# Full attention layers: one of a quad's 32 exponential tiles computed on VectorE and POOL instead of ScalarE

## The chip, the core and the metric

One core of a Trainium2 chip. The metric is the time of one launch in device microseconds. The engines are named as the profile names them: PE (matrix products), PEld (its weight loads), DVE (VectorE), ACT (ScalarE), POOL (GpSimd) and SP (SyncE, which issues the DMAs).

## What is computed

Four layers of pre-norm attention with a residual, on 2048 rows of width 512, 32 heads of width 16, all in float32: layers 0 and 2 look at the 256 rows up to their own (windowed), layers 1 and 3 at all rows (full).

```python
def _B_ref(x, wqkv, wo):            # _A_ref: the same with a mask of W = 256
    qkv = (lambda x, *d: x.transpose(*d))((x @ wqkv).reshape(B, S, 3, H, Dh), 2, 0, 3, 1, 4)
    q, k, v = qkv[0], qkv[1], qkv[2]
    scores = jnp.einsum("bhqd,bhkd->bhqk", q, k) * scale
    p = _softmax(scores, axis=-1)
    o = jnp.einsum("bhqk,bhkd->bhqd", p, v)
    return (lambda x, *d: x.transpose(*d))(o, 0, 2, 1, 3).reshape(B, S, D) @ wo

x = A_x
x = x + _A_ref(_layernorm(x, axis=-1), A_wqkv, A_wo)
x = x + _B_ref(_layernorm(x, axis=-1), B_wqkv, B_wo)
x = x + _A_ref(_layernorm(x, axis=-1), A_wqkv, A_wo)
x = x + _B_ref(_layernorm(x, axis=-1), B_wqkv, B_wo)
```

## The kernel before

The work of a full layer is cut into 32 quads: four blocks of 512 query rows (c) by eight groups of four heads (qd). Layer 1 takes the blocks one after the other with all eight groups of each; layer 3 takes two groups of every block, then the next two. A quad meets its 2048 keys in 16 steps j of 128 keys (`attn_full`, L767). A step makes two tiles of scores, one for each pair of heads: a tile is 128 keys by two heads by 512 queries, 128x1024 numbers.

- `exps` (L718): eight matmuls (L727) write a tile of scores into a PSUM buffer; there are two such buffers (`ps_s`). ACT takes the exponential into an SBUF tile e (L735); there are six of these (EB). A shift that keeps the exponent in range is part of the operands, as an added row of q and of k, so there is no running maximum.
- `pv` inside `attn_full` (L779): the value product of a step, called PV below, multiplies both tiles of the step with the values and adds into the two banks `acc`. A column of ones in the values gives the softmax's denominator.
- `epilogue` (L681): when a quad's last PV is done, DVE takes `acc` to SBUF (the tile sa, by `join`, L415 and L416), transposes, divides, and every second quad splits the result into two float16 halves (POOL takes one subtraction, L712). The next quad's first PV starts `acc` anew and so waits for sa.

Between these matmuls PE does **side work**: the projections of queries, keys and values, and the output product, of this layer or the next. They run as groups of eight matmuls of 64 rows (`mms`, L390, L399) into the one remaining PSUM bank pair, called halves, b in the rows of the profile. A chain of such groups (12 for a tile of 128x512 in most cases) ends with `join` on DVE, which frees the bank for the next chain. Query and key projections also square their result (POOL, L521), sum the squares (L543) and take a maximum (L562) or a shift (L575, L576).

The order of PE's and DVE's instructions in full layers is written by the program itself, in the order of a simulated clock kept in Python: a step counts 1.8 us, a group of side work MM = 0.222 us, DVE's backlog is kept in `vt_`. `share` (L949) deals out side work by a budget: after the second scores of a step one to two groups, as long as the clock allows. Light DVE work is queued by `soon` and issued by `drain` when DVE is thought to be free. `flush` (L738) decides when a PV is emitted: a step's PV comes two steps' scores later, between the two scores of a step, because `attn_full` hands control back (`yield None`) after its first tile and `attention` (L986) then calls `flush(1)`. ACT's and SP's instructions are placed by the framework's scheduler.

A quad's operands are the query tile qt (two buffers, L748) and two halves of the keys kt (three buffers, L752); `attention` loads a quad's operands while the one ahead runs, but not across the end of a block.

The memory rings that matter below: `vw` has three buffers (VB) and holds side work's weights and layer 2's value tiles (L623); `xh` has four (XNB).

Of the kernel before, what the change touches and what calls it, by code (L numbers as in the profile page):

```python
# [33 lines left out]
EB, XB, XNB, WB, VB, OB = 6, 4, 4, 2, 3, 5  # L34
RINGS = WB, VB
L_MIN = 2.0 ** -90
# [153 lines left out]
def fast_path(ctx, tc, flag, a_x, a_wqkv, a_wo, b_wqkv, b_wo, out):  # L190
# [13 lines left out]
    ctx.push(ps_x)  # L204
    dp = pool("scr", 1, space=bass.MemoryType.DRAM)
# [5 lines left out]
    XC, XN, V, O, OT, KM, PH = {}, {}, {}, {}, {}, {}, {"free": 0.0, "busy": False}  # L211
    WT, ST, pend = {}, {}, []
    VQ, vt_ = [deque() for _ in range(4)], [0.0]
# [15 lines left out]
    def soon(chain, us, f):  # L229

        if PH["full"]:
            VQ[chain].append((clock[0], us, f))
        else:
            f()

    def drain(upto=None):

        if upto is not None:
            for q in VQ[:upto]:
                while q:  # L240
                    vec(q[0][1])
                    q.popleft()[2]()
            return
        while vt_[0] <= clock[0] + 0.2:
            q = next((q for q in VQ if q), None)
            if q is None:
                return
            vec(q[0][1])
            q.popleft()[2]()
# [21 lines left out]
    zeros = cp.tile([P, QC], F16, name="zeros")  # L271
# [15 lines left out]
    nc.gpsimd.memset(zeros, 0.0)  # L287
# [15 lines left out]
    def fill(t, key, c0=0, c1=1):  # L303
        r4 = lambda d0, d1: rows(t).rearrange("h (d b) (c n) -> h d b c n", b=4, n=QC)[:, d0:d1, 3]
        for c in range(c0, c1):
            if key:
                nc.sync.dma_start(r4(0, 1)[:, 0, c], ones[:H])
                nc.sync.dma_start(r4(1, DH)[:, :, c], zeros[:H, None, :].broadcast_to([H, DH - 1, QC]))
# [33 lines left out]
    def verify(ty, s):  # L342

        am = vp.tile([P, D], F32, name=f"wa{ty}_{s}", tag="wa", bufs=1)
        for k in range(NC):
# [4 lines left out]
            yield from turns(3, (1.1, lambda: nc.vector.tensor_reduce(am[:, f], raw.rearrange("p k f -> p f k"), axis=AX.X, op=ALU.max,  # L350
                                                                      apply_absolute_value=True)))

        def bounds():
            at = vp.tile([P, D], F32, name=f"wt{ty}_{s}", tag="wc", bufs=1)
            nc.vector.transpose(at, am)
            mx = vp.tile([P, D // 32], F32, name=f"wx{ty}_{s}", tag="wx")
            nc.vector.tensor_reduce(mx, at.rearrange("p (b r) -> p b r", r=32), axis=AX.X, op=ALU.max)
            nc.vector.tensor_tensor(wlow, wlow, mx, ALU.min)
            nc.vector.tensor_tensor(whigh, whigh, mx, ALU.max)
        yield from turns(3, (1.8, bounds))  # L360
# [12 lines left out]
    def phase(l):  # L373

        PH["full"], PH["win"] = l is not None and l % 2 == 1, l is not None and l % 2 == 0
# [53 lines left out]
    def norm(l, c, xs, tail=False):  # L429

        mv, y, nb, out = ST[l, c][1], [], [], []

        def scales():
            y.append(rsqrt(nc, vp, f"{l}_{c}", mv[:, :, 1]))
# [4 lines left out]
        def parts(i):  # L439
            xn = vp.tile([P, D], F32, name=f"xn{l}_{c}_{i}", tag="xn", bufs=1)  # L440
# [12 lines left out]
        yield from turns(2, (2.4, scales), *[(1.8, lambda i=i: parts(i)) for i in range(4)])  # L453
# [24 lines left out]
    def project(l, s, c, act, ht=None):  # L478
# [5 lines left out]
        xc = XC[l, c]  # L484
        if s == 0:
# [6 lines left out]
        for t in range(NHT) if ht is None else (ht,):  # L492
# [19 lines left out]
            def parts(t=t, sp=None if full else sp, j=j if full else None):  # L512
                if full:
                    sp = vp.tile([P, 2, QC], F16, name=f"sp{n}_{t}", tag="sp", bufs=3)
                    nc.vector.tensor_copy(sp[:, 0], j)  # L515
                    nc.vector.tensor_tensor(sp[:, 1], j, sp[:, 0], ALU.subtract)
                sq = vp.tile([P, QC], BF16, name=f"sq{n}_{t}", tag="sq", bufs=NHT)
# [47 lines left out]
    def queries(l, c, act, ht=None):  # L565
        sqs = yield from project(l, 0, c, act, ht)

        def rest():
# [3 lines left out]
            if l % 2:  # L572
                r = quarters(ht)
                if PH["full"]:
                    nc.vector.tensor_scalar(m[r], ph[r, 0], -0.515, None, op0=ALU.mult)  # L575
                    nc.vector.scalar_tensor_tensor(m[r], ph[r, 1], -0.515, m[r], op0=ALU.mult, op1=ALU.add)  # L576
                else:
                    nc.vector.tensor_scalar(m[r], ph[r], -0.515, None, op0=ALU.mult)
# [16 lines left out]
    def key_shift(l, ht=None):  # L595
# [6 lines left out]
        nc.vector.tensor_scalar(m[r], ones[r], kx[r], -0.515, op0=ALU.mult, op1=ALU.mult)  # L602
# [4 lines left out]
    def values(l, c, act, halves=(0, 1), tiles=range(4)):  # L607
# [14 lines left out]
        else:  # L622
# [19 lines left out]
    def wo(l, c, tail):  # L642
# [17 lines left out]
        if PH["full"]:  # L660
            yield from norm(l + 1, c, xs, tail)
# [19 lines left out]
    def epilogue(l, c, qd, a):  # L681
# [33 lines left out]
        if u:  # L715
            soon(1, 1.2, parts)
# [524 lines left out]
```

## Time and profile before

| | |
|---|---|
| median of 3 runs | 2761.76 us (2757.35 to 2763.62) |
| the profiled execution | 2759.5 us, of which the span from the first to the last instruction 2757.7 us |
| busy in that span | PE 2496.1, ACT 2362.9, DVE 1094.9, PEld 1100.3, POOL 515.8 us |
| granted TensorE clock | 0.988 of full |
| layer 1, layer 3 | from about 500 to 1448 us, from about 1790 to 2741 us |
| DMA | 359.67 MB, mean 130 GB/s |

A row of the profile's groups reads: line, engine, operation, tile written <- tiles read, partitions x elements, count | busy time, mean length of one in ns | idle time of the engine in front of them, and what ended it. A row of the order of time reads: start, length, engine, line, operation, tiles, count, and in brackets the idle time ahead with what ended it; rows of one kind that follow each other without a break are merged, so "x8 ... 0.41" is eight matmuls from the start of the first to the end of the last. PE's matmuls overlap; the time that a group takes is read from start to start.

### The profile page before, as it was taken

The numbers are of one execution on the slowest core, as the hardware profiler recorded it, in microseconds if no ns is written. First come the engines' busy times: TensorE is split into PE (matmuls) and PEld (weight loads), VectorE is DVE, ScalarE is ACT, GpSimd is POOL, SyncE is SP. The second block draws the span as 40 slices with busy tenths as digits, with TensorE's granted clock in tenths as the row PEclk, the third lists the DMA queues.
The fourth block names the chain that finished last, engine by engine and source line by source line (L and its number), as shares of the span: only waits on it lengthen the run. The fifth ranks groups of instructions, "written<-read, shape, count | busy, mean of one in ns | idle before, by whom it ended". The sixth has DMA issues, their size and how long they took to land.

```text
span 2757.7 us, 112292 instructions
## 1 busy us (share of the span) xinstructions
PE 2496.1 (91%) x50513; PEld 1100.3 (40%) x50513; DVE 1094.9 (40%) x2314; ACT 2362.9 (86%) x2683; POOL 515.8 (19%) x1074
## 2 busy tenths in 40 slices
PE   7888989999989999999998898899899999998987
PEld 3233334444433344444443333534444444433332
DVE  5564554122343335325326566323333333333333
ACT  4556654899999999999995667399999999999997
POOL 1445552001000000100105678100000000000000
PEclk9999999999999999999999999999999999999999
DMA  8888856322342224324225565623232333333332
GB/s 286 226 241 240 244 178 191 96 83 82 100 120 79 86 93 137 102 78 126 93 73 169 157 181 143 175 72 109 84 107 90 98 97 104 112 104 123 114 120 103
DMA packets 335035, 359.67 MB, mean 130 GB/s; under 512 B 113616, under 2 KB 250320, under 8 KB 328144
## 3 DMA queue, kind: packets, MB, share of 16 engines
q1 hardware_dynamic: 334544, 352.40, 42.3%
q8 instruction: 397, 6.50, 1.0%
q14 instruction: 94, 0.77, 0.1%
HBM read 239.60 MB, written 96.99 MB: 122 GB/s over the span
## 4 chain that ended last, share of the span: by engine, by line
ACT 56%; PE 23%; issue 11%; DVE 5%; DMA 3%; POOL 2%; SPq 0%; ACTq 0%; DVEq 0%; POOLq 0%
ACT e L735 55%; PE b L402 10%; PE acc L812 3%; PE acc L779 3%; PE bs L402 2%; PE s L731 2%; PE s L727 2%; PE b L399 1%; POOL e L802 1%; POOL e L805 1%; DMA qt<-qs 1%; DMA kt<-kw 0%; DMA wr<-in_A_wo_dram 0%; DVE ot L694 0%; DMA w<-wd 0%
## 5 line engine op out<-in xcount | busy, mean ns | idle before, releaser
L735 ACT ACTIVATE e<-s 128x1024 f32<-128x1024 f32 (+2 forms) x2432 | 2238.8, 1058 | 121.0 <-PE s L731 95.3
L779 PE MATMUL acc<-e,vt 64*17 64x512 f32 x16384 | 1085.0, 590 | 1.3 <-issue 1.3
L727 PE MATMUL s<-qt,kt 64*32 64x512 f16 x16384 | 849.0, 380 | 130.4 <-ACT e L735 106.6
L727 PEld LDWEIGHTS <-kt 64*32 64x32 f16 x16384 | 406.7, 89 | 944.2 <-issue 868.8
L779 PEld LDWEIGHTS acc<-e,vt 64*17 64x17 f32 x16384 | 280.5, 92 | 61.1 <-issue 1.5
L805 POOL TENSOR_SCALAR_AFFINE_SELECT e<-e 128x256 f32<-128x256 f32 x512 | 224.9, 446 | 196.5 <-ACT e L735 195.4
L802 POOL TENSOR_SCALAR_AFFINE_SELECT e<-e 128x256 f32<-128x256 f32 x448 | 198.1, 449 | 114.1 <-ACT e L735 112.3
L712 POOL TENSOR_TENSOR oh<-o,oh 128x512 f16<-128x512 f32 x31 | 36.1, 1165 | 938.1 <-DVE oh L711 884.8
L812 PE MATMUL acc<-e,vt 128*17 128x384 f32 (+2 forms) x2816 | 204.7, 396 | 5.3 <-POOL e L802 4.0
L731 PE MATMUL s<-qt,kt 64*128 64x384 f16 (+2 forms) x1408 | 129.0, 280 | 64.0 <-ACT e L735 38.2
L415 DVE TENSOR_SCALAR sa<-acc 128x512 f32<-128x512 f32 x64 | 44.3, 692 | 335.4 <-PE acc L779 335.4
L402 PE MATMUL b<-xc,w 128*128 128x512 f16 x696 | 166.1, 390 | 7.0 <-DMA w<-wd 5.8
L677 DVE SCALAR_TENSOR_TENSOR x<-b,x 128x512 f32<-128x512 f32 x122 | 83.9, 688 | 193.0 <-PE b L399 189.8
L402 PEld LDWEIGHTS <-w 128*128 128x128 f16 x816 | 77.4, 100 | 122.8 <-issue 35.8
L521 POOL TENSOR_TENSOR sq<-sp 128x512 bf16<-128x512 f16 x28 | 41.0, 1463 | 442.2 <-DVE sp L515 427.6
L506 ACT ACTIVATE sp<-b 128x512 f16<-128x512 f32 x58 | 34.7, 598 | 103.3 <-PE b L402 91.2
L731 PEld LDWEIGHTS <-kt 64*128 64x128 f16 x1408 | 54.4, 94 | 167.6 <-issue 137.0
L521 POOL TENSOR_TENSOR sq_h<-sp_h 128x512 bf16<-128x512 f16 x27 | 40.1, 1484 | 409.8 <-DVE sp_h L515 409.8
L399 PE MATMUL b<-wo,oh 64*32 64x512 f16 x2592 | 109.9, 376 | 6.2 <-DVE x L677 3.1
L399 PE MATMUL b<-xc,w 64*32 64x512 f16 x2688 | 110.9, 376 | 3.0 <-DVE j L416 2.3
L399 PE MATMUL b<-xc,w_h 64*32 64x512 f16 x2592 | 104.4, 376 | 4.1 <-DVE km L562 3.9
L415 DVE TENSOR_SCALAR j_h<-b 128x512 f32<-128x512 f32 x27 | 18.7, 691 | 218.7 <-PE b L399 187.6
(136 smaller groups left out, 1874.8 us busy)
## 6 DMA issues: line engine op xcount, KB each, us to landing
kt<-kf SPq DMA_DIRECT2D x128, 512.0 KB
qt<-qs SPq DMA_DIRECT2D x128, 256.0 KB
xd<-x SPq DMA_DIRECT2D x96, 256.0 KB
x<-xd SPq DMA_DIRECT2D x96, 256.0 KB
w<-wd SPq DMA_DIRECT2D x22, 1024.0 KB
kt<-kw SPq DMA_DIRECT2D x64, 256.0 KB
qs<-sp SPq DMA_DIRECT2D x48, 256.0 KB
wo<-wd SPq DMA_DIRECT2D x12, 1024.0 KB
```

What stands on the lines that cost most here:

```text
L399: nc.tensor.matmul(ps[g:g + 32, r], a[k, g:g + 32], b[k], start=(i == 0), stop=(i == len(pairs) - 1), skip_group_check=True)
L402: nc.tensor.matmul(ps, a, b, start=(i == 0), stop=(i == len(pairs) - 1))
L415: nc.vector.tensor_scalar(dst, ps[0], scale, None, op0=ALU.mult)
L521: nc.gpsimd.tensor_tensor(sq, sp[:, 0], sp[:, 0], ALU.mult)
L677: nc.vector.scalar_tensor_tensor(xs[i], p, 1 / WS, xs[i], op0=ALU.mult, op1=ALU.add)
L727: nc.tensor.matmul(ps[g:g + 32, h], kt[R * h:R * h + R, pr, kc + g:kc + g + 32], qt[R * h:R * h + R, pr], start=True, stop=True, skip_grou ...
L731: nc.tensor.matmul(ps[:, h, s0:s0 + wd_], kt[R * h:R * h + R, pr, kc:kc + P], qt[R * h:R * h + R, pr, qc:qc + wd_], start=True, stop=True)
L735: nc.scalar.activation(e[:, :, w0:w1], ps[:, :, w0:w1], AF.Exp, scale=SCALE)
L779: nc.tensor.matmul(acc[r][32 * h:32 * h + DH + 1, :], V[l, qd // 4, j // 8][k, j % 8, 4 * (qd % 4) + h, :], es_[h // 2][k, h % 2, :], star ...
L802: nc.gpsimd.affine_select(v, v, pattern=[[0, 2], [-1, P]], compare_op=ALU.is_gt, fill=0.0, base=0, channel_multiplier=1)
L805: nc.gpsimd.affine_select(v, v, pattern=[[0, 2], [1, P]], compare_op=ALU.is_ge, fill=0.0, base=0, channel_multiplier=-1)
L812: nc.tensor.matmul(a[32 * h:32 * h + DH + 1, q * P:(q + nb) * P], V[l, (4 * c + j) // 4][:, j % 4, 4 * qd + h, :], es_[h // 2][:, h % 2, s ...
```

## The change

One tile of each quad, the first head pair of step 7 (`DJ`), no longer goes through ACT. It is called a unit. Its scores are written into the side work's bank (`unit`). DVE takes them from there, scaled by log2(e) and as whole numbers with 23 binary places, into an SBUF tile d; then it cuts out the fraction (two operations into a scratch tile) and the exponent bits (in place in d). POOL evaluates a polynomial of degree five in the fraction, ten operations for each half of 512, in five pieces, and multiplies d by it. The program decides in `units` when a unit is issued: at the earliest 6 us of its clock after its operands' load, when POOL has little left. The shift of the scores is changed so that they stay negative (L605 after the change).

Step 7 is moved to the end of the quad, so that its PV finds d ready. In the moved step only the second pair goes through ACT.

Further parts:
- e has five buffers in full layers instead of six (`EB = (6, 5)`); d has two.
- The scratch tile of the polynomial takes a buffer of `vw` in layer 1 and all of `xh` in layer 3. In layer 1 no unit is issued once layer 2's third value tile begins (`PH["off"]`).
- POOL's order, too, is written by the program in full layers (`PQ`, `pt_`).
- The next quad's operands are loaded across the end of a block (`fetch`).
- The planner: projections wait until the squares of the one ahead are due (`PH["sq"]`), up to two or three groups of side work between scores (`share`), and the split of the output waits for a free buffer (`OFREE`).
- The test of the weights' range is done in four pieces of 128 columns.

```diff
-EB, XB, XNB, WB, VB, OB = 6, 4, 4, 2, 3, 5
+EB, XB, XNB, WB, VB, OB = (6, 5), 4, 4, 2, 3, 5
+DJ = NT // 2 - 1
+TS, TT = 0.6, 1.25
+XP = 10 * (TS + TT)
...
+            if PH["full"] and c == 2:
+                PH["off"] = True
+                finish_unit()
             vt = V[l, c] = wp.tile([P, 4, H, DH + 1], F32, name=f"vt{n}", tag="vw", bufs=VB)
...
+    def unit(u):
+
+        ps = PH["halves"]
+        for g in range(0, P, 32):
+            for h in range(2):
+                nc.tensor.matmul(ps[g:g + 32, h], u["kt"][R * h:R * h + R, 0, DJ % 8 * P + g:DJ % 8 * P + g + 32],
+                                 u["qt"][R * h:R * h + R, 0], start=True, stop=True, skip_group_check=True)
+        spent(0.27)
+        vec(1.4)
+        PH["free"] = max(clock[0] + 0.6, vt_[0])
+        t = PH["ep"].tile([P, 2, QC], I32, name=f"d{u['n']}", tag="d", bufs=2)
+        nc.vector.tensor_scalar(t, ps, SCALE * LOG2E * 2.0 ** 23, -2.0 ** 30, op0=ALU.mult, op1=ALU.max)
...
+        def bits():
+            for h in range(2):
+                nc.vector.tensor_scalar(f[h].bitcast(I32), t[:, h], 0x7FFFFF, 0x3F800000, op0=ALU.bitwise_and, op1=ALU.bitwise_or)
+            nc.vector.tensor_scalar(t, t, 0x3F800000, None, op0=ALU.bitwise_and)
+            pt_[0] = max(pt_[0], vt_[0])
+            for k in range(5):
+                PQ.append((2 * (TS + TT), lambda k=k: horner(k)))
+
+        def horner(k):
+            for h in range(2):
+                if k:
+                    nc.gpsimd.tensor_scalar(a[h], a[h], POLY[4 - k], None, op0=ALU.add)
+                else:
+                    nc.gpsimd.tensor_scalar(a[h], f[h], POLY[5], POLY[4], op0=ALU.mult, op1=ALU.add)
+            for h in range(2):
+                if k < 4:
+                    nc.gpsimd.tensor_tensor(a[h], a[h], f[h], ALU.mult)
+                else:
+                    nc.gpsimd.tensor_tensor(x[:, h], a[h], x[:, h], ALU.mult)
+                    u["done"] = True
...
     def attn_full(l, c, qd, kt, qt, a):
-        for j in range(NT):
+        js = [j for j in range(NT) if j != DJ] + [DJ]
+        for j in js:
             es_ = []
-            for pr in range(2):
+            if j == DJ:
+                u = UX.popleft()
+                es_ = list(u["e"])
+                if es_:
+                    finish_unit() if UX and not UX[0]["e"] or not UX else None
+            PH["step"] = 1.8 - 0.9 * len(es_)
+            for pr in range(len(es_), 2):
                 es_.append(exps(f"{l}_{c}_{qd}_{j}_{pr}", kt[j // 8], qt, pr, [(j % 8 * P, 0, QC, 0)]))
                 if pr == 0:
                     yield None
...
-            self.lag = max(self.lag - 0.42, -0.3)
+            self.lag = max(self.lag - 0.48, -0.4)
...
-                   and self.spent - s0 < 1.5 * MM):
+                   and self.spent - s0 < (1.5 if self.lag > 0.1 else 2.5) * MM):
```

How it moves instructions, at three places. The first is PE at the end of a quad of layer 1 (s_1_2_15_1: scores of block 1, quad 2, step 15, pair 1; s_1_3_0_0: the next quad's first). One row of each group of eight or four matmuls is shown. Before:

```order
L727 MATMUL s_1_2_15_1_13728<-qt_1_2_12382,kt_1_2_1_12386 32x512
L727 MATMUL s_1_3_0_0_13745<-qt_1_3_13088,kt_1_3_0_13090 32x512
L779 MATMUL acc_81<-e_1_2_14_0_13678,vt_0_1_5232 17x512
L727 MATMUL s_1_3_0_1_13769<-qt_1_3_13088,kt_1_3_0_13090 32x512
L779 MATMUL acc_81<-e_1_2_15_0_13713,vt_0_1_5232 17x512
L727 MATMUL s_1_3_1_0_13793<-qt_1_3_13088,kt_1_3_0_13090 32x512
```

And after the change, at the same place:

```order
L767 MATMUL s_1_2_15_1_13888<-qt_1_2_12564,kt_1_2_1_12568 32x512
L767 MATMUL s_1_2_7_1_13923<-qt_1_2_12564,kt_1_2_0_12566 32x512
L767 MATMUL s_1_3_0_0_13950<-qt_1_3_13245,kt_1_3_0_13247 32x512
L892 MATMUL acc_81<-e_1_2_14_0_13842,vt_0_1_5228 17x512
L892 MATMUL acc_81<-e_1_2_15_0_13878,vt_0_1_5228 17x512
L767 MATMUL s_1_3_0_1_13987<-qt_1_3_13245,kt_1_3_0_13247 32x512
L892 MATMUL acc_81<-d_1_2_12947,vt_0_0_4499 17x512
L892 MATMUL acc_81<-e_1_2_7_1_13932,vt_0_0_4499 17x512
L767 MATMUL s_1_3_1_0_14011<-qt_1_3_13245,kt_1_3_0_13247 32x512
```

Step 7's one score tile stands between step 15's and the next quad's, and two PVs (of steps 14 and 15) stand between the next quad's first two score tiles, where one stood. This is so at all 31 places between two quads of a full layer.

The second place is PE at the end of layer 1 (quad 3_7 is its last; s_0_0_0_0 is layer 2's first score tile). Before:

```order
L727 MATMUL s_3_7_15_1_28645<-qt_3_7_27293,kt_3_7_1_27297 32x512
L779 MATMUL acc_81<-e_3_7_14_0_28605,vt_1_1_5653 17x512
L779 MATMUL acc_81<-e_3_7_15_0_28635,vt_1_1_5653 17x512
L731 MATMUL s_0_0_0_0_28701<-qt_0_0_28694,kt_0_0_28693 128x384
```

After; the rows left out are 288 matmuls of layer 2's third value projection, b<-wv_2_0_0,xc_2, in three chains:

```order
L767 MATMUL s_3_7_15_1_29212<-qt_3_7_27838,kt_3_7_1_27842 32x512
L767 MATMUL s_3_7_7_1_29223<-qt_3_7_27838,kt_3_7_0_27840 32x512
...
L892 MATMUL acc_81<-e_3_7_14_0_29163,vt_1_1_5656 17x512
L892 MATMUL acc_81<-e_3_7_15_0_29202,vt_1_1_5656 17x512
L892 MATMUL acc_81<-d_3_7_28184,vt_1_0_5831 17x512
L892 MATMUL acc_81<-e_3_7_7_1_29232,vt_1_0_5831 17x512
L771 MATMUL s_0_0_0_0_29585<-qt_0_0_29578,kt_0_0_29577 128x384
```

The projection that ran among the quads of layer 1 now stands for the most part behind their last scores.

The third is POOL, which runs a unit's chain without other work in between (here layer 3's second one; scr_0 and scr_1 hold the fraction, scr_2 and scr_3 the polynomial); DVE's part of another unit stands below it:

```order
L808 TENSOR_SCALAR scr_2_33926<-scr_0_33924 128x512
L808 TENSOR_SCALAR scr_3_33927<-scr_1_33925 128x512
L811 TENSOR_TENSOR scr_2_33926<-scr_2_33926,scr_0_33924 128x512
L811 TENSOR_TENSOR scr_3_33927<-scr_3_33927,scr_1_33925 128x512
L806 TENSOR_SCALAR scr_2_33926<-scr_2_33926 128x512
L806 TENSOR_SCALAR scr_3_33927<-scr_3_33927 128x512
...
L813 TENSOR_TENSOR d_0_1_34497<-scr_2_33926,d_0_1_34497 128x512
L813 TENSOR_TENSOR d_0_1_34497<-scr_3_33927,d_0_1_34497 128x512
L551 TENSOR_TENSOR sq_1_0_h_1_34999<-sp_1_0_h_1_34996 128x512
```

```order
L789 TENSOR_SCALAR d_1_4_46951<-b_33923 128x1024
L797 TENSOR_SCALAR scr_0_33924<-d_1_4_46951 128x512
L797 TENSOR_SCALAR scr_1_33925<-d_1_4_46951 128x512
L798 TENSOR_SCALAR d_1_4_46951<-d_1_4_46951 128x1024
```

Before, POOL had 46 and 42 operations in the two full layers; now each of their 64 quads has twenty more. A unit's scores stand 29 to 56 score tiles ahead of the PV that uses d, and two units of a layer stand 20 to 41 apart.

251 lines of the change are left out of this document (171 added, 80 removed).

## The prediction

> **What bounds the kernel now.** I read the page first, then stretches by layer, then the order of time around one quad boundary in a full layer. The page:
>
> ```profile
> span 2757.7 us, 112292 instructions
> PE 2496.1 (91%) x50513; PEld 1100.3 (40%) x50513; DVE 1094.9 (40%) x2314; ACT 2362.9 (86%) x2683; POOL 515.8 (19%) x1074
> ACT 56%; PE 23%; issue 11%; DVE 5%; DMA 3%; POOL 2%; SPq 0%; ACTq 0%; DVEq 0%; POOLq 0%
> ```
>
> The stretches are layer 1 (full), the end of layer 1 with layer 2 (windowed), and layer 3 (full); columns are length, then busy time of PE, PEld, DVE, ACT, POOL.
>
> ```profile
> 500.00:1448.00 948.00, 885.96 (x22478) 399.17 (x22456) 320.24 (x640) 939.34 (x1020) 59.46 (x46) 1.00 0.31 94
> 1448.00:1790.00 342.00, 302.11 (x2945) 131.30 (x2949) 195.80 (x455) 207.54 (x260) 198.91 (x483) 0.98 0.57 166
> 1790.00:2741.00 951.00, 867.33 (x21550) 384.51 (x21534) 308.55 (x578) 938.59 (x1019) 57.52 (x42) 1.00 0.33 102
> ```
>
> In the full layers ACT works 99% of the time, DVE a third, POOL 6%. ACT looks like the limit, and its pace is one tile in 0.92 us: 181 tiles stand without a visible break in 166.63 us, and one quad's evacuation follows the last after 29.43 us (32 tiles).
>
> ```profile
> 959.68 166.63 ACT L735 ACTIVATE e<-s 128x1024 f32<-128x1024 f32 x181
> L735 ACT ACTIVATE e<-s x2432: 590/1085/1096, 54.0 to 2736.7; 128x1024 f32<-128x1024 f32 x180, 128x768 f32<-128x768 f32 x4, 128x512 f32<-128x512 f32 x4
> 1092.87 0.69 DVE L415 TENSOR_SCALAR sa<-acc 128x512 f32<-128x512 f32 x1
> 1122.30 0.69 DVE L415 TENSOR_SCALAR sa<-acc 128x512 f32<-128x512 f32 x1 [11.72 <-PE acc L779]
> ```
>
> (One ACTIVATE shows 1.085 us, 0.17 of it beside the next.) But PE is nearly as tight. This is one round of two tiles:
>
> ```profile
> 1039.00 0.41 PE L727 MATMUL s<-qt,kt 64*32 64x512 f16 x8 [0.35 <-ACT e L735]
> 1039.22 1.05 PE L779 MATMUL acc<-e,vt 64*17 64x512 f32 x16
> 1040.08 0.41 PE L727 MATMUL s<-qt,kt 64*32 64x512 f16 x8
> 1040.29 0.63 PE L399 MATMUL b<-wo,oh 64*32 64x512 f16 x16
> 1040.84 0.41 PE L727 MATMUL s<-qt,kt 64*32 64x512 f16 x8
> ```
>
> From start to start: scores 0.22, value product (PV) 0.86, scores 0.21, two side groups 0.43 and some waiting; 1.84 us for the two tiles, as on ACT. Scores have two PSUM buffers, so PE can't run ahead: it waits for ACT to free one (0.35 us in the first row). From scores to scores over one PV is 1.08 us, already above 0.92. So a late PE reaches ACT almost whole. The trace shows it where a side group waited 0.76 us for DVE:
>
> ```profile
> 1123.46 2.85 ACT L735 ACTIVATE e<-s 128x1024 f32<-128x1024 f32 x3
> 1125.89 0.63 PE L399 MATMUL b<-xc,w 64*32 64x512 f16 x16 [0.76 <-DVE j L416]
> 1126.32 0.41 PE L727 MATMUL s<-qt,kt 64*32 64x512 f16 x8
> 1126.49 1.48 POOL L521 TENSOR_TENSOR sq<-sp 128x512 bf16<-128x512 f16 x1 [16.04 <-DVE sp L515]
> 1126.85 3.93 ACT L735 ACTIVATE e<-s 128x1024 f32<-128x1024 f32 x4 [0.54 <-PE s L727]
> 1126.99 1.03 DVE L698 TENSOR_TENSOR lmin<-lmin,ot 128x16 f32<-128x16 f32 x1
> ```
>
> ACT idled 0.54 us and lost its 0.17 of overlap: 0.71 of the 0.76.
>
> **The change part by part.** The built order holds 64 ACTIVATEs fewer, one in each of the 64 quads, so the change does what it says.
>
> *The tile off ACT.* 64 x 0.92 = -58.9 us, if PE can follow.
>
> *PE at the quad boundary.* PE does the same matmuls; the unit's scores go to the side work's bank. But tile pair 7 now stands last with one exponential, and the PV of pair 14 is held back by it. The order rows show scores, PV 14, PV 15, scores: between two scores stand 2 x 0.86 + 0.22 = 1.94 us, where 1.08 stood. The first of these scores waits for the buffer that the exponential of pair 15 frees, so PE can't have begun sooner, and there is no reserve ahead of it. The added 0.86 us falls on ACT: -0.92 + 0.86 = -0.06 a quad. **64 x -0.06 = -3.8 us** is what is left of 58.9. (Also 5 instead of 6 buffers for the exponentials: the next quad's first exponential then needs PV 14 done, which is sooner than the late scores; nothing more.)
>
> *Side groups.* Before, at most two stood between two scores. Now 121 such places hold three: 1.08 + 0.22 + 3 x 0.215 = 1.94 against 1.84 for a round, 0.1 late each. Bounds 0 and +12; those next to a boundary are already late, so I take +7.
>
> *End of layer 1.* The scratch tile takes a buffer of the ring that layer 2's third value tile needs, so that projection is put off behind the last unit: 288 of its matmuls, 36 groups, now run after the last scores, ahead of the last PVs. Before, the last scores and layer 2's first were 2.67 us apart:
>
> ```profile
> 1445.39 0.41 PE L727 MATMUL s<-qt,kt 64*32 64x512 f16 x8
> 1448.06 0.50 PE L731 MATMUL s<-qt,kt 64*128 64x384 f16 x4
> L415 DVE TENSOR_SCALAR vt<-b 128x512 f32<-128x512 f32 x12 | 8.2, 681 | 63.4 <-PE b L399 63.4
> L416 DVE SCALAR_TENSOR_TENSOR vt<-b,vt 128x512 f32<-128x512 f32 x12 | 8.3, 692 | 0.4
> ```
>
> 36 x 0.215 = 7.7, and twice between its three pieces PE waits for the one bank: 0.68 + 0.69 and some 0.3 of handing over, 1.7 each. **+11 us**, bounds 8 (pieces overlap) and 14.
>
> *VectorE.* A unit adds one operation of 128x1024 from PSUM and three on SBUF (one of 1024, two of 512). The nearest rows:
>
> ```profile
> L562 DVE TENSOR_REDUCE km<-b 128x1 f32<-128x1024 f32 x3 | 3.7, 1225 | 5.0 <-PE b L543 5.0
> L711 DVE CAST oh<-o 128x512 f16<-128x512 f32 x64 | 28.1, 439 | 2.2
> ```
>
> 1.23 + 2 x 0.44 + 0.88 = 3.0 us a quad (up to 3.8 if the last three run at the 0.69 of the 512-wide rows above), on an engine with 19 of 29 us free. The finer pieces of the weight test hide there too. After 33 units the next side group follows over only two scores and one PV; that round lasts 1.84 us, so 0.3 us of DVE being late there is a stall.
>
> *POOL.* Ten one-input and ten two-input operations of 128x512 a quad.
>
> ```profile
> L712 POOL TENSOR_TENSOR oh<-o,oh 128x512 f16<-128x512 f32 x31 | 36.1, 1165 | 938.1 <-DVE oh L711 884.8
> L521 POOL TENSOR_TENSOR sq<-sp 128x512 bf16<-128x512 f16 x28 | 41.0, 1463 | 442.2 <-DVE sp L515 427.6
> L805 POOL TENSOR_SCALAR_AFFINE_SELECT e<-e 128x256 f32<-128x256 f32 x512 | 224.9, 446 | 196.5 <-ACT e L735 195.4
> ```
>
> Two inputs: 1.17 (the f32 row is nearest) to 1.46. One input: between the half-size row, 0.45, and twice it, 0.89; I take 0.6. Together 17.7 us, upper end 23.5, and 1.9 of the old work: under 28.5 a quad. A unit is issued 29 to 56 tiles (27 to 51 us) before its PV, so the wait added on PE is covered. Two units can stand 20 tiles (18.4 us) apart; then VectorE's writing into the scratch may wait a few times for POOL.
>
> *POOL against VectorE.*
>
> ```profile
> L698 DVE TENSOR_TENSOR lmin<-lmin,ot 128x16 f32<-128x16 f32 x128 | 30.2, 236 | 3.2
> ```
>
> At 1126.99 above lmin, 16 elements wide, took 1.03 us and ended 0.05 us after POOL's sq; its mean over the kernel is 0.24 us. About ten small or two-input VectorE operations a quad now meet a POOL that is two thirds busy, where it was 6%. Their own length is hidden; only one in front of a join or the evacuation that PE waits for counts. Bounds 0 and +0.85 x 64 = +54; by the few places where such an operation stands right there, I take 0.1 a quad: +6.
> [...]
>
> *Loads across blocks.* There is nothing to gain in waiting for operands; PE's scores waited 0.8 us for them in all:
>
> ```profile
> L727 PE MATMUL s<-qt,kt 64*32 64x512 f16 x16384 | 849.0, 380 | 130.4 <-ACT e L735 106.6 <-DMA kt<-kf 0.8 <-issue 0.6
> PE b L399 <- DVE j L416: 3.0, 4, 0.8
> PE b L399 <- DVE km L562: 3.9, 3, 1.3
> SPq L752 <- PE s L727: 145.9, 27, 13.8
> ```
>
> Since pair 7 is last, the first key half stays in use to the quad's end and the next quad's second half loads later, needed only 14 tiles (13 us) on; SP's queue already waited up to 13.8 us there. The planner's new conditions on projections may take away some stalls behind DVE; the two rows above hold 7 us. -4, bounds 0 and -10.
>
> **Sum**, on the profiled execution (2759.5 us, 2757.7 of it span): -3.8 + 7 + 11 + 6 - 4 = +16, 2776. The median of the runs is 2.3 us above that execution: **2778 us**.
>
> **The rivals.**
> *The double PV is absorbed* (faster). If PE had 0.86 us in hand at the boundary, the whole 58.9 would come: 2759.5 - 58.9 + 7 + 11 + 6 - 4 + 2 = 2723. For it: PE's need without side work is 1.30 of each 1.84 us, so on average there is room. Against: room is no reserve with two score buffers, as the 0.76 us stall shows. It decides from 0.86 us of slack between the freed buffer and ACT's need. 0.13.
> *Stalls go and nothing is held* (near no change): -3.8 + 0 + 8 - 10 + 0 gives 2756 with the 2.3. 0.10, half of it under the bound.
> *POOL holds VectorE* (clearly slower): if in most quads an operation held by POOL stands ahead of the evacuation, 0.6 x 64 = 38 us instead of 6: 2810. It decides where VectorE, not PE, ends the boundary. For it: the evacuation and PE's next PV already touch each other. Against: POOL has 9 us free in a quad. 0.15.
>
> **How the numbers follow.** The forecast holds 0.62, of which 0.09 within 0.2% (5.5 us, about what a measurement of this kernel tells from no change) of 2761.8. Faster: 0.13 + 0.05 = 0.18; same: 0.05 + 0.09 = 0.14; slower: 0.53 + 0.15 = 0.68. The range 2750 to 2815 leaves out the first rival and the end of the last, some 0.18.
>
> **What would show it.** Right: quad spacing of about 29.4 us again, with ACT idle for 0.8 us (0.7 by the row) once in each quad, ended by the next quad's second scores; some 13 us between layer 1's last scores and layer 2's first; POOL busy 60 to 70% in full layers. Wrong: spacing near 28.5 (first rival); or idle ACT behind DVE evacuations, small VectorE operations of 0.5 us and more, and spacing above 30 (last rival).

## The result and the profile after

The changed kernel takes **2867.42 us** (median of 4 runs, 2864.99 to 2867.98), the kernel before 2759.56 us (4 runs, 2757.35 to 2763.62): a ratio of **1.0387, 95% interval 1.0369 to 1.0405**, slower by 108 us. The forecast was 2778 us with a range to 2815. Its direction was right, its size was not: 89 us are missing from its sum.

The page of the changed kernel: the span, the busy time of the engines, and the chain that ended last.

```profile
span 2866.0 us, 114018 instructions
PE 2515.1 (88%) x50513; PEld 1095.4 (38%) x50513; DVE 1478.5 (52%) x2671; ACT 2326.5 (81%) x2619; POOL 2192.3 (76%) x2354
...
ACT 34%; PE 24%; POOL 18%; issue 11%; DVE 10%; DMA 3%; SPq 1%; ACTq 0%; DVEq 0%; POOLq 0%
```

POOL went from 19% to 76% of the span, and in the chain it stands for 18% where it was 2%; DVE for 10% where it was 5%. The same by layer (layer 1, layer 3; columns as before: length, PE, PEld, DVE, ACT, POOL, then the granted clock):

```profile
500.00:1480.00 980.00, 888.03 (x22304) 394.06 (x22304) 530.07 (x859) 921.28 (x990) 897.83 (x688) 0.99 0.29 90
1850.00:2850.00 1000.00, 864.97 (x21134) 375.51 (x21133) 468.09 (x704) 904.44 (x967) 874.21 (x670) 0.98 0.32 98
```

In layer 1 POOL works 897.83 of 980 us, 92%, and in layer 3 87%; ACT fell from 99% to 94% and, in layer 3, to 90%. An engine that I had at 60 to 70% is nearly full. Its groups (line, operation, shape, count | busy us, mean ns | idle ahead):

```profile
L806 POOL TENSOR_SCALAR scr<-scr 128x512 f32<-128x512 f32 x512 | 781.7, 1535 | 20.9
L811 POOL TENSOR_TENSOR scr<-scr 128x512 f32<-128x512 f32 x256 | 328.1, 1303 | 7.7
...
L808 POOL TENSOR_SCALAR scr<-scr 128x512 f32<-128x512 f32 x128 | 91.9, 718 | 205.5 <-DVE scr L797 197.5
```

L806, the addition of a coefficient in place, takes 1.535 us on the mean; L808, with a multiplication and an addition in one instruction on the same shape, 0.718. A quad needs 8 x 1.535 + 2 x 0.718 + 10 x 1.30 = 26.7 us of POOL, and 1.9 of older work: 28.6 of the quad's 29.4.

An undisturbed quad still looks as forecast. This is one boundary in layer 1, in order of time (start, length, engine, line, operation; in brackets the idle time ahead). The scores are those of step 15, of step 7, and the next quad's first two:

```profile
827.86 0.41 PE L767 MATMUL s<-qt,kt 64*32 64x512 f16 x8
...
828.73 0.41 PE L767 MATMUL s<-qt,kt 64*32 64x512 f16 x8
...
829.54 0.41 PE L767 MATMUL s<-qt,kt 64*32 64x512 f16 x8
...
829.76 1.91 PE L892 MATMUL acc<-e,vt 64*17 64x512 f32 x32
...
830.92 7.77 ACT L775 ACTIVATE e<-s 128x1024 f32<-128x1024 f32 x8 [0.51 <-PE acc L892]
...
831.47 0.41 PE L767 MATMUL s<-qt,kt 64*32 64x512 f16 x8
```

The row of 32 matmuls is PV 14 and PV 15 together, 1.93 us from scores to scores, and ACT idles 0.51 us (0.68 with the 0.17 of overlap that it loses). From sa to sa most quads of layer 1 take 29.4 us (median 29.57); in layer 3 the median is 30.69. The end of layer 1 is as forecast too:

```profile
1476.90 0.41 PE L767 MATMUL s<-qt,kt 64*32 64x512 f16 x8 [0.35 <-ACT e L775]
...
1477.11 2.79 PE L424 MATMUL b<-wv,xc 64*32 64x512 f16 x96
...
1481.43 2.78 PE L424 MATMUL b<-wv,xc 64*32 64x512 f16 x96 [1.54 <-DVE vt L441]
...
1485.76 2.78 PE L424 MATMUL b<-wv,xc 64*32 64x512 f16 x96 [1.54 <-DVE vt L441]
...
1491.05 0.50 PE L771 MATMUL s<-qt,kt 64*128 64x384 f16 x4
```

Three times 96 matmuls with two waits of 1.54 us: 14.15 us between the two scores, where it was 2.67, so 11.5 more, where 11 were forecast. What was not forecast stands in PE's waits (waiting line <- who ended it: us in total, times, longest):

```profile
PE b L573 <- POOL sq_h L551: 31.3, 7, 9.2
...
PE b L783 <- DVE j L441: 8.8, 2, 6.1
PE b L424 <- DVE km L592: 8.1, 5, 2.7
PE b L424 <- DVE x L712: 7.6, 11, 1.0
PE b L424 <- DVE j L441: 6.7, 1, 6.7
```

All seven waits for squares stand in layer 3. Before, the longest wait for VectorE or POOL in the full layers was 1.5 us. The longest one now, with POOL's queue ahead of it:

```profile
2679.14 3.06 POOL L806 TENSOR_SCALAR scr<-scr 128x512 f32<-128x512 f32 x2
...
2679.47 0.56 DVE L544 CAST sp_h<-j_h 128x512 f16<-128x512 f32 x1
...
2695.82 1.05 POOL L551 TENSOR_TENSOR sq_h<-sp_h 128x512 bf16<-128x512 f16 x1
...
2696.92 0.61 PE L573 MATMUL b<-sq_h,hsum 64*32 64x512 bf16 x2 [9.17 <-POOL sq_h L551]
```

The square's input is ready at 2680.0; the square itself starts 15.8 us later, behind the rest of a unit's polynomial, which the planner (it counts 0.6 us for each addition, as I did) believed done. PE stands with the hsum matmuls at the head of its queue, and all scores behind them.

This wait is followed by slow matmuls. These are 10 us around its end, and the 10 us after them:

```profile
2690.80:2701.00 10.20, 4.08 (x64) 1.74 (x71) 1.39 (x2) 2.33 (x3) 10.20 (x9) 0.50 0.10 27
2701.00:2711.20 10.20, 9.27 (x226) 3.81 (x211) 6.27 (x13) 10.01 (x12) 1.95 (x4) 1.00 0.45 147
```

The granted clock of the first stretch is 0.50, and a PV in it takes 1.71 us from start to start, where it takes 0.86 a little later. The full layers of the changed kernel have 14 stretches at 0.50, 65 us in all, in which PE works 47 us; each begins during a wait of PE of 2 us or more, or within 1.3 us after one. The full layers of the kernel before have neither such a wait nor such a stretch, and my sum had no term for them. What they add to the waits themselves isn't separated.

### The profile page after: what moved, and what is told of

It is laid out like the page before. It is cut to its first block, busy times and chain, and to the rows that moved or that the text cites. A ratio compares the mean times of both kernels' runs of the same rounds, so it can differ in the third digit from the quotient of the medians.

```text
span 2866.0 us, 114018 instructions
## 1 busy us (share of the span) xinstructions
PE 2515.1 (88%) x50513; PEld 1095.4 (38%) x50513; DVE 1478.5 (52%) x2671; ACT 2326.5 (81%) x2619; POOL 2192.3 (76%) x2354
## 4 chain that ended last, share of the span: by engine, by line
ACT 34%; PE 24%; POOL 18%; issue 11%; DVE 10%; DMA 3%; SPq 1%; ACTq 0%; DVEq 0%; POOLq 0%
ACT e L775 33%; PE b L427 9%; POOL scr L806 8%; POOL scr L811 7%; PE acc L892 4%; PE acc L925 3%; PE s L767 2%; PE bs L427 2%; PE s L771 2%; PE b L424 2%; POOL scr L808 1%; DVE xh L475 1%; DVE xn L469 1%; POOL e L918 1%; POOL e L915 1%
## 5 line engine op out<-in xcount | busy, mean ns | idle before, releaser
L775 ACT ACTIVATE e<-s 128x1024 f32<-128x1024 f32 (+2 forms) x2368 | 2202.9, 1043 | 265.7 <-PE s L771 111.8
L767 PE MATMUL s<-qt,kt 64*32 64x512 f16 x15872 | 835.9, 383 | 142.5 <-ACT e L775 114.4
L806 POOL TENSOR_SCALAR scr<-scr 128x512 f32<-128x512 f32 x512 | 781.7, 1535 | 20.9
L767 PEld LDWEIGHTS <-kt 64*32 64x32 f16 x15872 | 381.3, 90 | 892.7 <-issue 813.2
L811 POOL TENSOR_TENSOR scr<-scr 128x512 f32<-128x512 f32 x256 | 328.1, 1303 | 7.7
L811 POOL TENSOR_TENSOR scr<-scr,scr 128x512 f32<-128x512 f32 x256 | 326.0, 1294 | 7.7
L808 POOL TENSOR_SCALAR scr<-scr 128x512 f32<-128x512 f32 x128 | 91.9, 718 | 205.5 <-DVE scr L797 197.5
L813 POOL TENSOR_TENSOR d<-scr,d 128x512 f32<-128x512 f32 x128 | 166.0, 1317 | 0.0
L789 DVE TENSOR_SCALAR d<-b 128x1024 int32<-128x1024 f32 x64 | 78.2, 1221 | 80.5 <-PE b L783 76.1
L424 PE MATMUL b<-xc,w_h 64*32 64x512 f16 x2592 | 108.7, 383 | 10.4 <-DVE km L592 6.8
```

The source lines that it names most:

```text
L424: nc.tensor.matmul(ps[g:g + 32, r], a[k, g:g + 32], b[k], start=(i == 0), stop=(i == len(pairs) - 1), skip_group_check=True)
L767: nc.tensor.matmul(ps[g:g + 32, h], kt[R * h:R * h + R, pr, kc + g:kc + g + 32], qt[R * h:R * h + R, pr], start=True, stop=True, skip_grou ...
L775: nc.scalar.activation(e[:, :, w0:w1], ps[:, :, w0:w1], AF.Exp, scale=SCALE)
L806: nc.gpsimd.tensor_scalar(a[h], a[h], POLY[4 - k], None, op0=ALU.add)
L811: nc.gpsimd.tensor_tensor(a[h], a[h], f[h], ALU.mult)
L813: nc.gpsimd.tensor_tensor(x[:, h], a[h], x[:, h], ALU.mult)
```

## The experiments

**1. The form of POOL's addition.**

```diff
-nc.gpsimd.tensor_scalar(a[h], a[h], POLY[4 - k], None, op0=ALU.add)
+nc.gpsimd.tensor_scalar(a[h], a[h], POLY[4 - k], 1.0, op0=ALU.add, op1=ALU.mult)
```

> The one-operation addition of the polynomial (8 a quad) is written as (a + c) * 1.0, two operations in one instruction; same value, same place, nothing else changed. Theory 'price of POOL': the one-operation form takes 1.49 us where I had 0.6, the two-operation form took 0.62 alone; POOL then needs 10 x 0.72 + 10 x 1.3 + 1.9 = 22 us of a 29.4 us quad instead of 28.7, and the time falls to where my forecast stood: 2770 to 2790 us, POOL 70 to 75% busy in the full layers, quad spacing 29.4. [...] Rival 'planner and loads': 2850 or more, since neither is touched.

Measured: 2814.20 us (2811.90 to 2817.12), ratio 1.0194 (1.0177 to 1.0211). POOL's groups:

```profile
L806 POOL TENSOR_SCALAR scr<-scr 128x512 f32<-128x512 f32 x512 | 319.8, 625 | 41.8
...
L808 POOL TENSOR_SCALAR scr<-scr 128x512 f32<-128x512 f32 x128 | 101.7, 795 | 342.3 <-DVE scr L797 337.0
```

The same addition with a second, idle operation falls from 1.535 to 0.625 us, and the kernel gains 53 us. The price theory holds for these 53, but the time stays 36 us above the forecast and 24 above the expectation's 2790: near the 2810 of the prediction's last rival, though its spacing above 30 us is seen in layer 3 alone (median 30.45; layer 1 29.58). More than one thing was wrong. From the first quad's sa to the last one's, layer 3 falls by 42.3 us (988.8 to 946.5) and layer 1 by 6.0 (961.0 to 955.0). No wait for squares is left, and the work that PE does at a clock of 0.50 falls from 47 to 25 us.

**2. One operation, or in place?** On top of experiment 1, in the polynomial's first operation:

```diff
-nc.gpsimd.tensor_scalar(a[h], f[h], POLY[5], POLY[4], op0=ALU.mult, op1=ALU.add)
+nc.gpsimd.tensor_scalar(a[h], f[h], POLY[4], None, op0=ALU.add)
```

> As e1_two_ops, but the polynomial's first operation, which reads one tile and writes another, has one operation (f + c) instead of two; this leaves out the multiplication by the leading coefficient. Theory 'one operation is the slow form': the first operation goes from about 0.7 to about 1.5 us, and the time to within 10 us of e1_two_ops. Rival 'in place is the slow form': the first operation stays at 0.7, and the additions in e1_two_ops stay at 1.5.

Measured: 2817.06 us in one run. The two forms have changed places:

```profile
L806 POOL TENSOR_SCALAR scr<-scr 128x512 f32<-128x512 f32 x512 | 321.8, 628 | 41.8
...
L808 POOL TENSOR_SCALAR scr<-scr 128x512 f32<-128x512 f32 x128 | 201.2, 1572 | 304.9 <-DVE scr L797 299.2
```

L808 reads one tile and writes another and still takes 1.572 us, where L806 in place takes 0.628. The form with one operation (an addition in both places) is the slow one; in place plays no part in that.

**3. The two value products at the boundary**, on top of experiment 1.

```diff
             PH["step"] = 1.8 - 0.9 * len(es_)
+            if es_:
+                yield None
```

> As e1_two_ops, and at a quad's last tile pair one value product more is issued before the single exponential's scores, so that products 14 and 15 no longer stand together between the next quad's first two score tiles. Theory 'double value product': the 0.86 us given back at the boundary goes in about 62 quads, 53 us below e1_two_ops: 2717 to 2737 us, spacing 28.5. Rival 'something else ends the boundary' (the evacuation on VectorE, or the buffers of the exponentials): within 10 us of e1_two_ops, spacing still 29.4.

Measured: 2768.29 us (2765.94 to 2770.96), ratio 1.0027 (1.0014 to 1.0040): 46 us below experiment 1, the quads' median 29.2 us. So the place was the right one, and it held 46 of the 53 us. (The 2717 to 2737 us of the expectation aren't met: they counted from a lower time for experiment 1.) Some 0.4 us a quad stay: a side group and a PV still stand together between two scores there.

**4. The change without its units.**

```diff
     def units():
-        for u in UX:
+        for u in ():
```

> No unit is issued: all 32 exponential tiles of a quad go through ACT again, and POOL and VectorE do none of them; the rest of the change is kept (planner's conditions, loads across blocks, pair 7 last, five buffers). Theory 'all of the change in time comes from the units': 2753 to 2766 us, as before within 0.25%, quad spacing 29.4. Rival 'planner, loads or five buffers cost': 2775 or more; rival 'they gain' (stalls behind VectorE gone): 2750 or less.

Measured: 2763.53 us (2760.02 to 2769.30), ratio 1.0015 (1.0006 to 1.0025), the quads' median 29.5 us. Planner, loads, order of steps and the five buffers together cost 3 us; that they gain is ruled out.

**5. The units without the polynomial**, on top of experiment 3, so that POOL is as free as before and all other instructions stand in the same order:

```diff
         def horner(k):
-            for h in range(2):
-                if k:
-                    nc.gpsimd.tensor_scalar(a[h], a[h], POLY[4 - k], 1.0, op0=ALU.add, op1=ALU.mult)
-                else:
-                    nc.gpsimd.tensor_scalar(a[h], f[h], POLY[5], POLY[4], op0=ALU.mult, op1=ALU.add)
-            for h in range(2):
-                if k < 4:
-                    nc.gpsimd.tensor_tensor(a[h], a[h], f[h], ALU.mult)
-                else:
-                    nc.gpsimd.tensor_tensor(x[:, h], a[h], x[:, h], ALU.mult)
-                    u["done"] = True
+            if k == 4:
+                u["done"] = True
```

> As e2_boundary, with POOL's twenty operations of a unit left out (the polynomial isn't computed, so one tile in 32 holds a power of two only); the order of all other instructions is the same. Theory 'POOL holds VectorE': in e2_boundary VectorE's operations beside POOL run up to three times as long (the three of the normalization 0.55, 0.54, 0.69 us alone and 1.39, 1.49, 1.65 beside it), and this is why PE waits for VectorE's x, m, j, vt and sa (20 us in all) and part of why the boundaries aren't smooth; without POOL those waits fall to some 5 us and the time to 2735 to 2755 us, spacing 28.7 to 29.0. Rival 'VectorE's own new work and the order': waits and time stay, 2762 or more.

Measured: 2747.11 us (2741.89 to 2757.20), ratio 0.9961 (0.9946 to 0.9976), 21 us below experiment 3; the quads' median 29.08 us. What went is seen in experiment 3's rows, in the normalization of one block of rows, the first part beside POOL, the last with POOL idle:

```profile
1313.44 2.76 POOL L811 TENSOR_TENSOR scr<-scr 128x512 f32<-128x512 f32 x2
1313.56 1.49 DVE L469 TENSOR_SCALAR xh<-x,mv,y 128x512 f16<-128x512 f32 x1
...
1315.09 1.66 DVE L475 TENSOR_TENSOR xh<-xn,xh 128x512 f16<-128x512 f32 x1
...
1319.01 0.54 DVE L469 TENSOR_SCALAR xh<-x,mv,y 128x512 f16<-128x512 f32 x1
1319.58 0.69 DVE L475 TENSOR_TENSOR xh<-xn,xh 128x512 f16<-128x512 f32 x1
...
1320.19 0.68 DVE L440 TENSOR_SCALAR j<-b 128x512 f32<-128x512 f32 x1
...
1321.66 1.15 PE L424 MATMUL b<-xc,w 64*32 64x512 f16 x24 [3.55 <-DVE j L441]
```

The same two operations take 1.49 and 1.66 us beside POOL's multiplications and 0.54 and 0.69 without. Each is off the path; but the join j, which frees PE's side bank, stands behind them on VectorE, and PE waits 3.55 us. VectorE's groups over the whole kernel, of experiment 3:

```profile
L742 DVE TENSOR_TENSOR op<-ot,r 128x256 f32<-128x256 f32 x128 | 72.6, 568 | 4.1
...
L798 DVE TENSOR_SCALAR d<-d 128x1024 int32<-128x1024 int32 x64 | 63.2, 987 | 2.2
...
L441 DVE SCALAR_TENSOR_TENSOR sa<-acc,sa 128x512 f32<-128x512 f32 x64 | 44.3, 692 | 7.4 <-PE s L767 0.9
...
L749 DVE CAST oh<-o 128x512 f16<-128x512 f32 x64 | 40.8, 637 | 2.2
```

and of experiment 5:

```profile
L742 DVE TENSOR_TENSOR op<-ot,r 128x256 f32<-128x256 f32 x128 | 58.1, 454 | 4.1
...
L798 DVE TENSOR_SCALAR d<-d 128x1024 int32<-128x1024 int32 x64 | 44.4, 694 | 2.2
...
L749 DVE CAST oh<-o 128x512 f16<-128x512 f32 x64 | 28.0, 438 | 2.2
```

Multiplications, additions and casts from SBUF to SBUF grow, with one input as well as with two; sa, which reads PSUM, keeps 0.692 us in both. VectorE's transposes (0.71 us) and reductions (1.08 us) keep their length too, though they go from SBUF to SBUF.

The time is the theory's, its mechanism in part: PE's waits for x, m, j, vt and sa fall from 20.8 to 10.4 us, not to 5. Those for j and sa, most of them behind normalizations, are gone; those for m (4.4 us) and vt (3.1) stay.

**6. The other terms together: the changed kernel's own order, without the polynomial** (the edit of experiment 5 on the changed kernel).

> The changed kernel's order, with POOL's twenty operations of a unit left out (the polynomial isn't computed) and nothing else altered: PE, ACT and VectorE do what they do in the changed kernel, and POOL is free. This tests the other terms of the recorded sum together: without the term for POOL holding VectorE they give 2772 us. Theory 'the other terms are right': 2766 to 2778 us, quad spacing 29.4, and all of the miss is POOL (its price and its hold). Rival 'they are too small as well': e5_no_poly plus what the boundary cost between e1_two_ops and e2_boundary, 2747 + 46 = 2793 us, from 2785 up.

Measured: 2786.71 us (2783.33 to 2792.93), ratio 1.0102 (1.0081 to 1.0123), against 2772 and 2793: the rival. In layer 1 most quads stand at 29.4 us and the 31 together take 929.1 us, 7.5 more than before with the end of the layer in it: there my sum holds (some 11). In layer 3 they take 946.3, which is 21 more, in which I had about nothing. A third of its quads last 30.4 to 30.6 us, like this one, just past its boundary:

```profile
2195.84 0.38 PE L573 MATMUL b<-sq_h,hsum 64*32 64x512 bf16 x2
...
2196.69 0.69 DVE L441 SCALAR_TENSOR_TENSOR sa<-acc,sa 128x512 f32<-128x512 f32 x1
...
2198.16 0.68 DVE L605 TENSOR_SCALAR m<-b 32x512 f16<-32x512 f32 x1
...
2198.88 0.68 DVE L606 SCALAR_TENSOR_TENSOR m<-b,m 32x512 f16<-32x512 f32 x1
...
2199.62 0.84 PE L424 MATMUL b<-xc,w_h 64*32 64x512 f16 x24 [0.89 <-DVE m L606]
```

The matmuls of the squares stand right behind the quad's last PV, VectorE takes sa first, and the next side group waits 0.89 us for m with the scores behind it. Such waits for m, x and km were 1.6, 3.1 and 3.9 us in the full layers before; here they are 6.1, 4.5 and 8.2, those for km up to 2.3 us at a time, as VectorE is then in a unit's own operations. Three quads with such a wait for km take 33.9 to 34.9 us (31.5 before), and right behind it the granted clock is 0.50 for 3.4 us, which these layers don't show before.

Set against experiment 1, this run says where POOL's work at the lower price costs: in layer 1, which falls from 955.0 to 929.1 us, and there 24.2 of the 25.9 us come from four quads, the three in which a normalization stands and the one behind the first of them. In the first of these PE waited 6.3 us for sa, which stood on VectorE behind the normalization's twelve operations. Layer 3 has no normalization, and although POOL works 68% of it in experiment 1, it takes 946.5 and 946.3 us.

**7. The boundary's edit alone**, on the changed kernel with its slow additions.

> The changed kernel with the edit at the boundary alone (the order of e2_boundary); POOL's additions stay in the form of one operation. Theory 'POOL sets the pace of the changed kernel' (28.7 us of POOL a quad): the edit that was worth 46 us with the cheap additions is worth less than half of it here, 2845 to 2862 us; PE's waits that end at POOL or behind VectorE grow in its place. Rival 'the terms add': 2867 - 46, 2815 to 2828 us.

Measured: 2840.71 us (2836.40 to 2842.91), ratio 1.0295 (1.0280 to 1.0311): 27 us below the changed kernel where it was worth 46, neither theory's number. POOL works 895.94 of 970 us in layer 1, and the largest new wait is there still:

```profile
PE b L573 <- POOL sq_h L551: 33.9, 8, 8.2
```

So the terms don't add while POOL is full, but a full POOL isn't a floor that cancels the gain either.

**8. The end of layer 1 dealt with by the planner**, on top of experiment 3, and then two conditions of the planner more.

```diff
-sd = sd or Side(NT * NQD // 2, works[0], works[1], 0.33)
+sd = sd or Side(NT * NQD // 2, works[0], works[1], 0.4)
...
-sd = Side(NT * NQD * NQ - NT * NQD // 2, works[1], works[2], 0.33)
+sd = Side(NT * NQD * NQ - NT * NQD // 2, works[1], works[2], 0.4)
```

> As e2_boundary, with layer 1's least share of side work per step at 0.40 instead of 0.33, so that no side matmul stands behind layer 1's last scores (288 did); three of the 64 units then go through ACT again. Theory 'end of layer 1': the 12.4 us without an exponential after the last scores fall to some 2.7, and three tiles of 0.92 come back: 7 us less than e2_boundary, 2758 to 2764 us. Rival 'the side work only moves its stall into the quads': 2766 or more.

Measured: 2779.40 us (2776.05 to 2780.82), ratio 1.0069 (1.0052 to 1.0086): 11 us slower than experiment 3, so the rival is right. The side work left the end of the layer and came to stand in bursts inside it, where the normalizations that follow it meet POOL:

```profile
PE acc L894 <- DVE sa L440: 12.0, 3, 8.9
...
PE b L424 <- DVE j L441: 9.7, 3, 8.2
```

Two of layer 1's quads last 39.5 us and more. The second edit:

```diff
-            if PQ or VQ[2] or PH["off"] or pt_[0] > clock[0] + 3.0:
+            if PQ or VQ[2] or PH["off"] or pt_[0] > clock[0] + 3.0 or pend and pend[0][0] < clock[0] + 4.0:
...
-                expect(l, c, qd, *held[0], 6.0)
+                expect(l, c, qd, *held[0], 9.0)
```

> As e9_tail; besides, a unit isn't issued when a reduction of squares (km, m) is due within 4 us, and an operand's earliest unit stands 9 us instead of 6 after its load. Theory 'units in front of km, and early units': PE's waits for km (8.8 us, 2.7 at a time, VectorE being in the unit's d and bits) fall to about 3, those for the operand's DMA (3.8 us) go: 8 to 12 us less than e9_tail. Rival: nothing gained, as the waits only move to other side groups: within 3 us of e9_tail.

Measured: 2768.38 us (2764.79 to 2772.86), ratio 1.0034 (1.0020 to 1.0048), 11 us below the last. The time is the theory's, the mechanism only in part: the units' waits for their operand fell from 4.8 to 0.7 us, but km's are 8.2 us as before. Where the rest came from stays open.

**9. The polynomial on VectorE**, on top of the first edit of experiment 8. VectorE adds and multiplies in one instruction:

```diff
-                PQ.append((2 * (TS + TT), lambda k=k: horner(k)))
+                for h in range(2):
+                    soon(4, 0.75, lambda k=k, h=h: horner(k, h))
...
+            if not k:
+                nc.vector.tensor_scalar(a[h], f[h], POLY[5], POLY[4], op0=ALU.mult, op1=ALU.add)
+            y = a[h] if k < 4 else x[:, h]
+            nc.vector.scalar_tensor_tensor(y, a[h], POLY[4 - k] if k else 0.0, f[h] if k < 4 else y, op0=ALU.add, op1=ALU.mult)
...
-            if PQ or VQ[2] or PH["off"] or pt_[0] > clock[0] + 3.0:
+            if PQ or VQ[2] or VQ[4] or PH["off"] or pt_[0] > clock[0] + 3.0:
```

> As e9_tail, with the polynomial on VectorE instead of POOL, in twelve pieces, addition and multiplication in one instruction (10 of some 0.69 and 2 of some 0.3 to 0.45 us a quad, 7.7 us), in the queue of the lowest priority; 62 units. Theory 'POOL holds VectorE': although VectorE takes 7.7 us more a quad (it had 16 of 29 free), PE's waits for it fall, since nothing holds it: spacing 28.7 to 29.0, 2725 to 2745 us. Rival 'VectorE's queue': each piece in front of an evacuation costs as much as POOL's hold did: 2755 us or more.

Measured: 2744.64 us (2743.41 to 2750.44), ratio **0.9952 (0.9935 to 0.9968)**: 35 us below its base, and 0.5% faster than the kernel before. Layer 1's stretch:

```profile
500.00:1440.00 940.00, 877.00 (x22560) 400.83 (x22551) 628.17 (x1207) 919.38 (x993) 62.65 (x49) 1.00 0.31 94
```

VectorE works 628 of 940 us, 67%, where it had 54% in the changed kernel, and PE's longest wait for it in the full layers is 2.3 us. So the polynomial costs less in VectorE's own queue, at 0.72 us an operation, than on POOL, where operations of 1.3 us hold VectorE. The edit also brings a unit's twenty operations down to twelve and moves them in the order, and these parts aren't separated; but 22.7 of the 24.4 us that layer 1 gains come from the quads with normalizations and those right behind them.

**10. The rest of the boundary**, on top of 9: in layer 3 no side group ahead of the single exponential; then with the second edit of experiment 8 as well.

```diff
+                    elif u == NT - 2 and (l == 3):
+                        sd.k += 1
                     elif u:
                         sd.step()
```

> As e7_poly_dve, and in layer 3 no side group is placed between the last two scores ahead of the single exponential (it stood there with a value product, 1.5 us between two scores for 0.92 of ACT). Theory 'PE at the boundary': the last idle time there, some 0.43 us in each of 31 quads, goes: 13 us less in layer 3 at most, 2731 to 2738 us in all. Rival 'the side groups take the time elsewhere in the quad': within 3 us of e7_poly_dve.

> As e10_no_side_l3, with the two planner conditions of e8_tail_km (no unit when a reduction of squares is due within 4 us; an operand's earliest unit 9 us after its load). They were worth 11 us there. Theory 'they add': 5 to 10 us less than e10_no_side_l3, since km's waits (6.9 us) and the operand's (3 us) are what is left to gain. Rival: within 3 us of it.

Measured: 2744.71 us (2740.08 to 2749.06), ratio 0.9954 (0.9941 to 0.9968), and 2741.45 us (2737.20 to 2742.69), ratio **0.9935 (0.9921 to 0.9948)**. The first edit gains nothing: undisturbed quads of layer 3 take 28.5 to 28.6 us, as without it, and the side groups that were moved make new waits (for the joins of vt, 4.5 us where there were 0.4; two quads last 33.7 and 34.2 us, where the longest were 33.1 and 33.6). The second is 3 us below it, less than I expected, and the two versions' runs overlap; km's waits, which it was to shorten, are 6.9 us as in experiment 9. It is the fastest version here, 17 us below the kernel before, out of the 57 that 62 units take off ACT.

## Why the prediction was wrong

The 89 us between 2778 and 2867 come apart in three, by experiments that differ in one thing each: 2867.4 - 2814.2 = 53 (the form of the addition), then 2814.2 - 2786.7 = 27.5 for POOL's work at the lower price where I had 6, so 21 more, then 2786.7 - 2772 = 15 in the other terms. The kernel before was not equally fast beside each of them (2759.6, 2760.2, 2756.8 us, and 2761.8 behind the forecast); counted from these, the miss is 92 and the parts are 54, 18 and 20.

- **The step that failed: "One input: between the half-size row, 0.45, and twice it, 0.89; I take 0.6."** It measured 1.49 us in the median and 1.535 on the mean, above the upper bound. The bounds were drawn by size alone, from an operation of another kind; nothing in the trace of before showed this form. With it fell "under 28.5 a quad" (23.5 and 1.9 at most; it is 28.6) and so the cover: POOL was full, and its squares, which I had not looked at as work that PE waits for, stood behind the polynomial. 53 us. Most of it shows as PE waiting for POOL itself: 42.3 of the 48.3 us that the two full layers gave back with the cheap form lie in layer 3, where all 31.3 us of waits for squares stood, and 3.4 more for POOL's oh.
- **POOL against VectorE** was named with bounds 0 and +54 and taken at 6; all of POOL's work at the lower price is 27.5, of which PE's waits for POOL itself are next to nothing. "Their own length is hidden; only one in front of a join or the evacuation" was the right mechanism. The third rival had the right kind of place, but not "in most quads": sa reads PSUM and isn't held itself (0.692 us with and without POOL's work), and it stood behind held operations in one quad of experiment 1. What I missed is that held operations come in bursts, the twelve of a normalization, with a join or sa behind them: three bursts in layer 1 carry nearly all of the cost, and the boundaries of layer 3 next to none. Operations with one input were held as well (CAST 0.438 to 0.637 us, L798 0.694 to 0.987, from experiment 5 to experiment 3), those that read PSUM weren't (the unit's d 1.224 us in both, like sa).
- **Planner, loads: "-4"** was the wrong sign: +3 without units (experiment 4, which has the other parts of the change in it as well), and with them the waits for m, x and km, most of them in layer 3, add about 10 us that no term held. The order put those for m right behind the boundary, where VectorE is with sa, and units in front of km; I had read the order there for PE's side only. This covers about half of layer 3's 21 us; the clock of 0.50 behind the waits for km may hold another part, and the rest is open. VectorE's operations of a unit take 2.8 us without POOL's work, as forecast (3.0), and 3.8 in the changed kernel. (The recorded upper end of 3.8 is 4.0 by the rows that it names.) The +7 for side groups wasn't tested by itself.
- **Right:** the boundary (-0.92 + 0.86: 29.4 us again in undisturbed quads, 0.68 us of idle ACT; taking the cause away gained 46 of the 53 us), and the end of layer 1 (+11; it measured 11.5).
- The range's upper end, 2815, left out the case in which POOL becomes the bound; its price was worked out only for the lower cost of an addition.

What isn't settled: how the rest of the 53 us divides between POOL's longer hold on VectorE (L797, which takes the fraction out on VectorE, lasts 0.74 us on the mean beside the slow form and 0.45 beside the cheap one) and the clock of 0.50; what the last part of the 15 to 20 us is; and which wait the second edit of experiment 8 took away.

## What to carry to other kernels

An operation that the trace of before doesn't show in its very form (engine, number of operations, number of inputs) has no bound from its neighbours (here 1.535 us against a bound of 0.89): measure it alone, or carry a price at which its engine is full into the range. Work moved to an idle engine is paid twice where it makes another engine's operations longer, as POOL's did with VectorE's here (0.54 us became 1.49): look for what stands in one queue behind a burst of held operations, not for the held ones. And before an engine is called free, list who waits for its old work, since that now stands behind the new.

## What the hardware showed

- POOL's TENSOR_SCALAR on 128x512 f32 takes 1.535 us with one operation in place (the changed kernel) and 1.572 from one tile to another (experiment 2); with two it takes 0.625 us in place (experiment 1) and, on the mean, 0.718 (the changed kernel) to 0.795 (experiment 1) from one tile to another.
- Beside POOL's two-input operations (1.30 us), VectorE's multiplications, additions and casts from SBUF to SBUF took up to two to three times as long (0.54 to 1.49, 0.69 to 1.66 in experiment 3's normalization); its transposes (0.71) and reductions (1.08), and those that read PSUM (0.69), kept their length.
- During or right behind waits of PE of 2 us and more the granted TensorE clock fell to 0.50 for 3.4 to 10.2 us, 14 times in the changed kernel's full layers, and a PV took 1.71 instead of 0.86 us; behind a wait of 2.66 us it stayed at 1.00. In the kernel before, whose waits stay under 1.6 us there, it didn't.
